# Attention and two feed-forward layers on one core: Q and K of eight tiles as whole rows, memory scores as own products, a new order

## The chip, the cores and the metric

The kernel runs on one core of one Trainium2 chip. The metric is the device time of one execution in microseconds (us). Engines are named as in the profile: PE is TensorE's matmul, PEld its weight load, DVE is VectorE, ACT is ScalarE, POOL is GpSimd, and SP is the engine whose queue issues most of the transfers.

## What is computed

Chunked attention with memory keys on q, k, v of 4 batches x 8 heads x 768 positions x 64, then two feed-forward layers on 3072 tokens x 512, with a hidden width of 2048.

```
for c in range(S // 32):
    k_full = concat(mem_k (8 keys), k[32c - 16 : 32c + 32 + 8])
    v_full = concat(mem_v, v[the same])
    a = softmax(q[chunk c] @ k_full.T / 8)
    out[chunk c] = a @ v_full
x = out as (3072, 512)
x = softplus(x @ w_in) @ w_out
h = x @ w2_in
out = (max(h, 0) + alpha * min(h, 0)) @ w2_out
```

## The kernel before

**Numbers.** All dense products are exact to about float32: each operand is split into a high and a low part in PE's float32r format, and a product is high x high + high x low + low x high. The weights come as 64-bit doubles (`load_raw`, tile `raw`, 512 KB each) and are turned into float32 (tile `word`) by integer operations on DVE: `magnitude` (ab), `clamp` (cl), `convert_a`, `convert_b`, `convert_c` (ca, cb, cv). A high part is then a cast on ACT (wh), and a low part a subtraction on DVE (wl), into `wsplit`.

**Tiles and steps.** Attention is cut into 24 tiles of 128 queries (t = 0 to 23). A tile has scores on PE (`a_scores`, s, into `ps_s` or, from tile 8 on, `ps_a`), a row maximum (m), a shift or bias (c) and an exp (e, on ACT), a sum (n), its reciprocal (r) and the scaling (w), a transpose on PE (t) with its copy (pt, on ACT), the products with V (v*), and a high and a low part of the result (xh on ACT, xl on DVE) into the tile `x`. Four tiles make a block of 512 tokens. The first layer then runs in 96 steps: step i is `h i` (12 products of `x` with a weight block into `ps_hh`, tile `wsplit`), a softplus on ACT (sp, tile `ta`), its high and low part (hi on ACT, lo on DVE, tile `g`), and for the first 64 steps `out i` (12 products into `ps_o`). Steps 0 to 3 use block 0, so `h 0` needs the four tiles 0 to 3; steps 4 to 7 use block 1. Tiles 8 to 23 run between later steps. In the same stretch the weights of layer 2 are converted (ab2, cl2, cv2), split and stored back to memory. From about 495 us on the second layer follows, with seven block products in place of eight (`ps_q`).

**The loads of a tile.** In memory, row p of `qk[t]` holds for one of 128 partitions 1024 floats for Q and 4 x 160 for K: 6656 bytes. Partitions 0 to 63 hold even heads, 64 to 127 odd ones, and of the 1024 floats for Q only every second run of 64 is used, the other is zero. `load_q` (line 424) takes the used runs in two transfers of 64 partitions, `load_k` (line 429) K in a third. K's 160 columns hold the keys of two halves of a tile and the 8 memory keys in between (from column 88). `a_mem` (line 466, km) copies the memory keys on POOL to both ends of K's room, so that each chunk of 32 queries finds its 64 keys in one piece:

```
for e in range(2):
    pe.matmul(ps[at:at + CHUNK, g, u, :], lhsT=q[rows, ...],
              rhs=k_t[t][rows, g, KEYS[j]:KEYS[j] + KW], ...)
```

`load_v` (line 440) brings V of a tile in six transfers of 8, 56 or 64 rows.

**What sets the order.** Each engine's instructions are in a fixed order (`InOrder`). `schedule` (line 1102) gives every piece an engine, a cost, a due time, what it comes after and what rooms it takes; `Plan.run` (line 129) picks the next piece by due times, which are shifted by the offsets in the table `O`. For the opening, up to the sixth step, `OPENING` (line 96) writes the order out, engine by engine. Into PE's planned gaps of the first 90 us `keep_busy` (line 272) puts fillers, products of the zero tile that nobody reads. The planner charges 1.3 us for a change between the exp and the softplus table on ACT, for the pieces that name a table.

Of the kernel before, what the change touches and what calls it, by code (L numbers as in the profile page):

```python
# [11 lines left out]
ALU = mybir.AluOpType  # L12
# [21 lines left out]
MEM0 = SW - NMEM  # L34
KEYS = (0, NMEM + CHUNK, NMEM + 2 * CHUNK, KN - KW)
# [36 lines left out]
class InOrder:  # L72
# [5 lines left out]
    def __getattr__(self, name):  # L78
# [14 lines left out]
O = {'km': -67.99, 's': 76.27, 'm': 79.39, 'c': 26.14, 'e': 113.6, 'n': -26.07, 'r': -9.25, 'w': -103.69, 't': 93.99, 'pt': 7.83, 'v': -16.75, 'xh': 47.66, 'xl': -21.96, 'first': 40.59, 'gap': 81.03, 'second': -74.43, 'gap2': -33.65, 'raw': -107.74, 'ab': 35.37, 'cl': -63.78, 'ca': 12.95, 'cb': 130.93, 'cc': -95.51, 'wh': 81.65, 'wl': 56.47, 'odd': 73.44, 'sp': -41.74, 'hi': 56.35, 'lo': 40.29, 'out': 11.14, 'wait': 0.13, 'sloads': -155.21, 'km0': -117.22, 'km1': 25.05, 's0': 21.36, 's1': 46.75, 'm0': -88.99, 'm1': 60.17, 'c0': 12.89, 'c1': -122.81, 'e0': 101.82, 'e1': -91.77, 'n0': 6.01, 'n1': -115.72, 'r0': 23.2, 'r1': 81.11, 'w0': 40.81, 'w1': -130.46, 't0': 13.18, 't1': -36.53, 'pt0': -117.94, 'pt1': 5.34, 'v0': 51.02, 'v1': -82.24, 'xh0': -60.84, 'xh1': -81.21, 'xl0': 64.94, 'xl1': 45.67, 'by0': -46.78, 'by1': 30.48, 'va': -12.2, 'vb': 88.29, 'vc': 56.73, 'vd': -102.87, 'ra': 33.94, 'rb': 14.7, 'rc': 127.17, 'wld': 105.54, 'dra': -108.27, 'ca0': 58.14, 'ca1': -5.43, 'so': -164.69, 'sq': -8.86, 'sr': -75.99, 'sc': -117.58, 'gn': 46.22, 'l2': -197.81, 'gh': -1.03, 'gl': 116.66, 'ev': -85.64, 'gs': -141.72, 'wo': 68.04, 'yo': 44.51, 'h4': 201.96, 'ac': 53.11}  # L93
# [16 lines left out]
        m 0, corners, c 0, m 1, m 2, n 0, r 0, ab 0, c 1, c 2, m 3, w 0, cl 0, n 1, c 3, r 1, ca 0, cb 0, ab 1, n 2, cl 1, cv 0, r 2, w 1,  # L110
        ca 1, n 3, ab 2, r 3, w 3, cb 1, cl 2, cv 1, ca 2, cb 2, w 2, xl 0, wl 0, m 4, c 4, cv 2, xl 1, n 4, r 4, wl 2, m 5, xl 3, c 5, xl
        2, ab 3, cl 3, wl 1, n 5, ca 3, cb 3, cv 3, r 5, m 6, c 6, lo 0, wl 4, ab 4, cl 4, m 7, ca 4, c 7, cb 4, n 6, cv 4, ab 5, cl 5, ca
        5, cb 5, r 6, cv 5, xl 4, wl 6, n 7, lo 1, ab 6, r 7, cl 6, xl 5, ca 6, wl 3, cb 6, ab 7, cv 6, cl 7, lo 2, ca 7, wl 5, cb 7, xl 6,
# [120 lines left out]
def attention_mlp_mlp_kernel(ctx: ExitStack, tc, qk, v, w1, w2, consts, out):  # L234
# [139 lines left out]
    def low_part(eng, t):  # L374
        eng.tensor_tensor(out=t[1], in0=t[1].bitcast(F32), in1=t[0].bitcast(F32), op=ALU.subtract)
# [30 lines left out]
    raw_q, k_t, v_t, st, s_room = {}, {}, {}, {}, {}  # L406
# [7 lines left out]
    def room_qk(t):  # L414
        if t < 2 * TB:
            room = wpool.tile([P, 4 * DM], F32, tag="w", name="qk0")
            raw_q[t] = room[:, :QN // 2]
            k_t[t] = room[:, QN:QN + NPAIR * KN].rearrange("p (g k) -> p g k", k=KN)
        else:
            room = apool.tile([P, QN // 2 + NPAIR * KN], F32, tag="qk", name="qk", bufs=1)  # L420
            raw_q[t] = room[:, :QN // 2]
            k_t[t] = room[:, QN // 2:].rearrange("p (g k) -> p g k", k=KN)

    def load_q(t, e):
        part = slice(e * D, (e + 1) * D)
        rows = qk[t][part, :QN].rearrange("p (n e k) -> p n e k", e=2, k=D)[:, :, e]
        sp.dma_start(out=raw_q[t][part].rearrange("p (n k) -> p n k", k=D), in_=rows)
# [50 lines left out]
    def a_scores(t):  # L478
        q = raw_q[t].rearrange("p (n k) -> p n k", k=D)
# [27 lines left out]
    def a_max(t):  # L507
# [6 lines left out]
        for rows, w, at, on in ((slice(0, D), 0, slice(NMEM, NMEM + LEFT), i == 0),  # L514
                                (slice(D, P), 1, slice(LEFT + CHUNK, LEFT + CHUNK + RIGHT), i == TPB - 1)):
# [586 lines left out]
    def schedule(when):  # L1102
# [64 lines left out]
        def tile(t, prev, due, step=None):  # L1167
            start, few = t < TB, t >= 2 * TB

            def when_due(k):  # L1170
                return O[k if few else k + "01"[t >= TB]]
# [291 lines left out]
```

## Time and profile before

| what | value |
|---|---|
| time, median of 3 runs | 1075.3 us (1073.28 to 1078.04) |
| the profiled execution | 1077.0 us, its span 1075.2 us |
| PE busy | 1052.6 us, 98% |
| DVE, ACT, POOL busy | 793.8, 559.4, 160.4 us (74%, 52%, 15%) |
| mean granted clock | 0.995 |
| read from and written to memory | 169.42 MB, 60.82 MB |
| chain that ended last | PE 93%, DMA 2%, SP's queue 2%, DVE 1% |

The span is the time from the first to the last instruction. A share is of the span. A line number says nothing here: every engine call runs through the helper in line 80, so rows are told apart by tile names (`ps_hh<-x,wsplit` is an h step). PE's granted clock is a share of 2.4 GHz.

### The profile page before, as it was taken

What the parts mean: (1) busy time and instruction counts of PE and PEld (TensorE: products, weight loads), DVE (VectorE), ACT (ScalarE), POOL (GpSimd) and SP (SyncE); (2) the same over time, 40 slices, a digit from 0 to 9 for tenths busy, and PEclk for the clock granted to TensorE, in tenths of its full rate; (3) what the DMA queues carried; (4) which work ended last, traced back from release to release, by engine and by line L of the source; (5) the groups of instructions that cost most, each with busy time, mean ns of one, the idle gap of its engine ahead of it and who ended that gap; (6) DMA issues with size and microseconds to landing.
All of it is one profiled execution on the core that took longest, in us unless ns stands there. A gap on an engine that the chain in (4) does not pass through costs nothing.

```text
span 1075.2 us, 18801 instructions
## 1 busy us (share of the span) xinstructions
PE 1052.6 (98%) x7229; PEld 860.0 (80%) x7233; DVE 793.8 (74%) x1318; ACT 559.4 (52%) x957; POOL 160.4 (15%) x178
## 2 busy tenths in 40 slices
PE   6899999999999999999999999999999999999998
PEld 3688888887878888878878888888888888888886
DVE  5899995876766788876467766769666879566976
ACT  3564444454543555553355565655465655456543
POOL 0110110431222442235420000000000000000000
PEclk8999999999999999999999999999999999999999
DMA  9876699978657576773999564899875999856804
GB/s 212 221 202 221 169 237 298 232 223 224 202 189 228 181 249 197 255 230 122 357 308 279 217 245 130 309 284 292 203 288 177 342 298 254 265 200 253 362 1 79
DMA packets 171705, 248.25 MB, mean 231 GB/s; under 512 B 79328, under 2 KB 123488, under 8 KB 162400
## 3 DMA queue, kind: packets, MB, share of 16 engines
q1 hardware_dynamic: 166736, 225.95, 65.0%
q0 software_dynamic: 4608, 20.97, 10.0%
q8 instruction: 57, 0.93, 0.4%
q14 instruction: 32, 0.26, 0.1%
q10 hardware_dynamic: 272, 0.13, 0.0%
HBM read 169.42 MB, written 60.82 MB: 214 GB/s over the span
## 4 chain that ended last, share of the span: by engine, by line
PE 93%; DMA 2%; SPq 2%; DVE 1%; issue 1%; ACT 0%; POOL 0%
PE ps_q L80 49%; PE ps_hh L80 24%; PE ps_o L80 16%; PE ps_a L80 3%; SPq L80 2%; DMA qk<-in_qk_dram 1%; DMA raw<-in_w_dram 1%; DMA v<-in_v_dram 1%; PE ps_x L80 0%; DVE g L80 0%; DVE pt L80 0%; PE ps_s L80 0%; ACT g L80 0%; DVE sm L80 0%; PE ps_t L80 0%
## 5 line engine op out<-in xcount | busy, mean ns | idle before, releaser
L80 PE MATMUL ps_q<-g,wout 128*128 128x512 f32 x1344 | 306.9, 390 | 0.8 <-DVE g L80 0.8
L80 PEld LDWEIGHTS ps_q<-g,wout 128*128 128x128 f32 x1344 | 251.9, 188 | 54.6 <-DVE g L80 2.3
L80 PE MATMUL ps_hh<-x,wsplit 128*128 128x512 f32 x1152 | 277.1, 393 | 0.2 <-DVE x L80 0.2
L80 PEld LDWEIGHTS ps_hh<-x,wsplit 128*128 128x128 f32 x1152 | 215.7, 189 | 47.3 <-issue 1.6
L80 PE MATMUL ps_q<-xop,win 128*128 128x512 f32 x1008 | 229.0, 389 | 0.0
L80 PEld LDWEIGHTS ps_q<-xop,win 128*128 128x128 f32 x1008 | 189.3, 188 | 39.2
L80 DVE TENSOR_TENSOR g<-gb,g 128x512 fp32r<-128x512 f32 x224 | 154.6, 702 | 56.2 <-ACT g L80 54.5
L80 ACT CAST g<-gb 128x512 fp32r<-128x512 f32 x224 | 133.0, 621 | 117.3 <-PE ps_q L80 94.9
L80 PE MATMUL ps_o<-g,wsplit 128*128 128x512 f32 x768 | 187.7, 394 | 0.0
L80 PEld LDWEIGHTS ps_o<-g,wsplit 128*128 128x128 f32 x768 | 142.5, 188 | 30.1
L80 ACT ACTIVATE ta<-ps_hh 128x512 f32<-128x512 f32 x88 | 52.6, 598 | 121.9 <-PE ps_hh L80 118.8
L80 DVE SCALAR_TENSOR_TENSOR word<-raw,word 128x512 int32<-128x512 int32 x128 | 94.6, 739 | 2.7
L80 DVE TENSOR_TENSOR g<-ta,g 128x512 fp32r<-128x512 f32 x64 | 49.8, 778 | 41.4 <-ACT g L80 41.3
L80 ACT ACTIVATE tp<-gb 128x512 f32<-128x512 f32 x48 | 30.4, 633 | 90.6 <-DVE gb L80 90.6
L80 DVE SCALAR_TENSOR_TENSOR gb<-gb,tp 128x512 f32<-128x512 f32 x48 | 33.2, 692 | 45.5 <-ACT tp L80 45.5
L80 POOL TENSOR_TENSOR wst<-word,wst 128x512 fp32r<-128x512 f32 (+2 forms) x40 | 44.6, 1119 | 138.6 <-ACT wst L80 129.6
L80 POOL DMA_DIRECT2D gb<-gb x16 | 13.8, 862 | 322.9 <-DVE g L80 302.3
L80 DVE TENSOR_SCALAR word<-word 128x512 int32<-128x512 int32 (+1 forms) x128 | 54.9, 438 | 1.7
L80 ACT CAST g<-ta 128x512 fp32r<-128x512 f32 x64 | 39.7, 621 | 26.5 <-PE ps_o L80 25.8
L80 ACT ACT_TABLE_LOAD x36 | 46.2, 1283 | 3.5 <-PE ps_hh L80 2.2
L80 DVE TENSOR_SCALAR word<-raw 128x512 int32<-128x512 int32 x64 | 39.1, 611 | 8.2 <-DMA raw<-in_w_dram 8.2
L80 POOL TENSOR_TENSOR wst<-wst 128x1024 fp32r<-128x1024 f32 x16 | 41.0, 2565 | 21.1 <-ACT wst L80 16.8
(98 smaller groups left out, 919.9 us busy)
## 6 DMA issues: line engine op xcount, KB each, us to landing
wout<-out_ops SPq DMA_DIRECT2D x42, 1024.0 KB
raw<-in_w_dram SPq DMA_DIRECT2D x64, 512.0 KB
win<-in_ops SPq DMA_DIRECT2D x24, 1024.0 KB
win<-in_ops SPq DMA_DIRECT2D x24, 768.0 KB
gb<-gb POOLq DMA_DIRECT2D x16, 1024.0 KB, 13.2
wout<-outs SPq DMA_DIRECT2D x14, 1024.0 KB
in_ops<-wst SPq DMA_DIRECT2D x24, 512.0 KB
outs<-wst SPq DMA_DIRECT2D x16, 512.0 KB
```

The source lines that it names most:

```text
L80: i = getattr(self.engine, name)(*args, **kw)
```

## The change

Tiles 0 to 7 load Q and K as whole rows, 128 x 6656 bytes in one transfer, zeros included (`load_rows`). K stays as it lies in memory, without room at the ends. For them the scores of the first and the last chunk of a tile become two products each, one with 56 keys and one with the 8 memory keys where they lie (`WINDOWS`); the copies on POOL go. V's rows and the masked columns follow the new order of keys. Tiles 8 to 23 load and multiply as before. Layer 2's magnitude moves from DVE to ACT (`magnitude_by_act`), POOL's low parts run in two halves, some of the planner's costs are others, and `O` and `OPENING` hold new values.

```
+FEW = KW - NMEM
+WINDOWS = (((0, 0, FEW), (FEW, MEM0, NMEM)), ((0, CHUNK, KW),), ((0, 2 * CHUNK, KW),), ((0, MEM0, NMEM), (NMEM, KT - FEW, FEW)))
...
+    def magnitude_by_act(layer, k):
+        m = words[layer, k] = tpool.tile([P, DM], F32, tag="word", name="word", bufs=3)
+        act.activation(out=m, in_=raws[layer, k][:, :, 1].bitcast(F32), func=AF.Abs)
...
     def low_part(eng, t):
-        eng.tensor_tensor(out=t[1], in0=t[1].bitcast(F32), in1=t[0].bitcast(F32), op=ALU.subtract)
+        for n in (slice(0, 2), slice(2, 4)) if eng is pool else (slice(0, 4),):
+            eng.tensor_tensor(out=t[1][:, n, :], in0=t[1][:, n, :].bitcast(F32), in1=t[0][:, n, :].bitcast(F32), op=ALU.subtract)
...
         if t < 2 * TB:
-            room = wpool.tile([P, 4 * DM], F32, tag="w", name="qk0")
-            raw_q[t] = room[:, :QN // 2]
-            k_t[t] = room[:, QN:QN + NPAIR * KN].rearrange("p (g k) -> p g k", k=KN)
+            room = rows_of[t] = wpool.tile([P, 4 * DM], F32, tag="w", name="qk0")
+            raw_q[t] = room[:, :QN].rearrange("p (n e k) -> p n e k", e=2, k=D)
+            k_t[t] = room[:, QN:QK].rearrange("p (g k) -> p g k", k=KT)
...
+    def load_rows(t):
+        sp.dma_start(out=rows_of[t][:, :QK], in_=qk[t])
...
-                        pe.matmul(
-                            ps[at:at + CHUNK, g, u, :], lhsT=q[rows, u * NPAIR + g, c * CHUNK:(c + 1) * CHUNK],
-                            rhs=k_t[t][rows, g, KEYS[j]:KEYS[j] + KW], start=True, stop=True,
-                        )
+                        for to, key, many in WINDOWS[j]:
+                            pe.matmul(
+                                ps[at:at + CHUNK, g, u, to:to + many], lhsT=q[rows, u * NPAIR + g, e, c * CHUNK:(c + 1) * CHUNK],
+                                rhs=k_t[t][rows, g, key:key + many], start=True, stop=True,
+                            )
...
-            add(("ab2", j), "DVE", 0.35, due - 1, lambda j=j: magnitude(1, halves[j]), [("raw2", j)] + ([("ab2", j - 1)] if j else []), ["word"])
+            add(("ab2", j), "ACT", 0.62, due - 1, lambda j=j: magnitude_by_act(1, halves[j]), [("raw2", j)] + ([("ab2", j - 1)] if j else []), ["word"])
...
-        qk 0 2, i raw 0, i v
-        0, i raw 1, i q 4 0, i q 4 1, i raw 2, i v 1, i qk 4 2, i q 5 0, i q 5 1, i v 3, i qk 5 2, i v 2, i raw 3, i q 6 0, i q 6 1, i qk 6
...
+        i qk 0 2, i qk 1 2, i qk 2 2, i raw 0, i qk 3 2, i cst, i raw 1, i v 1, i raw 2, i v 3, i qk 4 2, i v 0, i qk 5 2, i v 2, i raw 3, i
+        qk 6 2, i qk 7 2, i raw 4, i v 4, i raw 5, i v 5, i raw 6, i v 6, i raw 7, i v 7, i raw 8, i raw 9, i raw 10, i raw 11, i q 8 0, i q
```

**SP, the start of its queue.** `qk_103` is tile 0's room before and `qk_102` the change's; the other qk names are tiles 1 to 3, `raw` is a weight block, `cst` the constants, `v_116` the room of a tile's V. Before:

```order
L80 DMA qk_103<-in_qk_dram 64x8x64 x2
L80 DMA qk_103<-in_qk_dram 128x4x160
L80 DMA qk_101<-in_qk_dram 64x8x64
L80 DMA qk_100<-in_qk_dram 64x8x64
L80 DMA qk_101<-in_qk_dram 64x8x64
L80 DMA qk_100<-in_qk_dram 64x8x64
L80 DMA qk_101<-in_qk_dram 128x4x160
L80 DMA cst<-in_consts_dram 128x144
L80 DMA qk_102<-in_qk_dram 64x8x64 x2
L80 DMA qk_100<-in_qk_dram 128x4x160
L80 DMA qk_102<-in_qk_dram 128x4x160
L80 DMA raw<-in_w_dram 128x512
```

Now:

```order
L82 DMA qk_102<-in_qk_dram 128x1664
L82 DMA qk_103<-in_qk_dram 128x1664
L82 DMA qk_100<-in_qk_dram 128x1664
L82 DMA raw<-in_w_dram 128x512
L82 DMA qk_101<-in_qk_dram 128x1664
L82 DMA cst<-in_consts_dram 128x144
L82 DMA raw<-in_w_dram 128x512
L82 DMA v_116<-in_v_dram 56x512
```

Twelve transfers for four tiles became four, the first weight block stands ahead of tile 3's rows, and the second ahead of all of V. Further down, V comes in the order of tiles 1, 3, 0, 2, with the rows of tiles 4 and 5 in between.

**PE, the scores of tile 0.** Before, they are one run of products behind the fillers:

```order
L80 MATMUL ps_s<-zero 128x512
L80 MATMUL ps_s<-qk_103 32x64 x32
L80 LDWEIGHTS zero
L80 MATMUL ps_s<-zero 128x512
```

Now the end of tile 0's and the start of tile 1's:

```order
L82 MATMUL ps_s<-qk_102 32x64 x4
L82 MATMUL ps_s<-qk_102 32x8
L82 MATMUL ps_s<-qk_102 32x56
L82 MATMUL ps_s<-qk_102 32x8
L82 MATMUL ps_s<-qk_102 32x56
L82 LDWEIGHTS zero
L82 MATMUL ps_s<-zero 128x512
L82 MATMUL ps_s<-qk_103 32x56
```

32 products in the program became 48 a tile, and five fillers between tiles 0 and 1 became one.

**ACT, between two h steps of the middle.** `ta<-ps_hh` is a step's softplus, `g<-ta` its high part, `pt<-pt` a tile's exp. Before, around the first V products of tile 8:

```order
L80 ACTIVATE ta<-ps_hh 128x512
L80 CAST g<-ta 128x512
L80 CAST wst<-word 128x256
L80 ACT_TABLE_LOAD
L80 ACTIVATE pt<-pt 128x512
L80 ACT_TABLE_LOAD
L80 ACTIVATE ta<-ps_hh 128x512
```

Now, at the same place:

```order
L82 ACT_TABLE_LOAD
L82 ACTIVATE word<-raw 128x512
L82 ACT_TABLE_LOAD
L82 ACTIVATE ta<-ps_hh 128x512
L82 CAST g<-ta 128x512
L82 CAST wst<-word 128x256
L82 CAST x<-ps_a 128x4x128
L82 ACTIVATE ta<-ps_hh 128x512
L82 CAST g<-ta 128x512
L82 ACT_TABLE_LOAD
L82 ACTIVATE word<-raw 128x512
```

The magnitude (`word<-raw`) came to ACT, and the compiler put a table load ahead of it and one behind. ACT's whole list has 84 table loads, 36 before.

## Rows read from the trace of the kernel before

**Rows 1.** The page, busy us (share of the span) and instructions of each engine.
```profile
PE 1052.6 (98%) x7229; PEld 860.0 (80%) x7233; DVE 793.8 (74%) x1318; ACT 559.4 (52%) x957; POOL 160.4 (15%) x178
```
**Rows 2.** Waits of PE: us in total, times, longest.
```profile
PE ps_s L80 <- POOL qk L80: 5.3, 5, 2.0
PE ps_a L80 <- issue: 3.4, 2, 2.2
PE ps_s L80 <- issue: 3.1, 3, 2.6
```
**Rows 3.** Timeline of PE, 0 to 62: start, us, operation, [idle before].
```profile
6.46 1.12 PE L80 MATMUL ps_s<-qk 64*32 64x64 f32 x64 [2.04 <-POOL qk L80]
...
17.32 1.34 PE L80 MATMUL ps_s<-qk 64*32 64x64 f32 x52 [2.63 <-issue]
...
31.41 1.20 PE L80 MATMUL ps_x<-pt,v 128*64 128x64 f32 x32
...
38.98 2.79 PE L80 MATMUL ps_hh<-x,wsplit 128*128 128x512 f32 x11 [0.22 <-DVE x L80]
43.81 0.41 PE L80 MATMUL ps_s<-qk 64*32 64x64 f32 x12 [2.04 <-POOL qk L80]
...
45.52 4.40 PE L80 MATMUL ps_hh<-x,wsplit 128*128 128x512 f32 x12
...
55.34 3.02 PE L80 MATMUL ps_hh<-x,wsplit 128*128 128x512 f32 x12
```
**Rows 4.** Windows: stretch, length; PE, PEld, DVE, ACT, POOL busy; PEclk, DMA share, GB/s.
```profile
0.00:14.72 14.72, 10.14 (x219) 5.29 (x222) 4.00 (x13) 3.23 (x10) 1.87 (x14) 0.88 0.91 211
...
20.00:30.00 10.00, 8.02 (x93) 4.99 (x92) 9.79 (x26) 6.04 (x20) 1.12 (x2) 0.94 0.88 197
...
40.00:50.00 10.00, 7.76 (x95) 5.66 (x97) 7.56 (x16) 5.73 (x8) 2.16 (x5) 0.83 0.97 237
```
**Rows 5.** Windows chosen by what the DMA queue moved.
```profile
3.00:9.00 6.00, 3.62 (x71) 1.85 (x71) 1.29 (x4) 0.00 (x0) 0.35 (x2) 0.88 1.03 207
...
15.00:24.00 9.00, 6.35 (x72) 3.66 (x72) 6.84 (x20) 5.74 (x25) 0.00 (x0) 0.81 1.08 225
...
48.00:60.00 12.00, 12.00 (x169) 9.66 (x168) 9.86 (x21) 6.21 (x11) 1.23 (x1) 0.98 0.86 235
90.00:102.00 12.00, 12.00 (x55) 9.94 (x54) 11.93 (x25) 5.31 (x9) 0.00 (x0) 1.00 0.53 170
```
**Rows 6.** Timeline of SP, 0 to 40.
```profile
0.74 5.42 SPq L80 DMA_DIRECT2D qk<-in_qk_dram  x8
...
13.97 0.37 SPq L80 DMA_DIRECT2D raw<-in_w_dram  x1
```
**Rows 7.** Timeline of DVE, 0 to 40.
```profile
18.75 0.69 DVE L80 TENSOR_REDUCE nm<-ps_s 128x8 f32<-128x512 f32 x1 [2.02 <-PE ps_s L80]
19.36 0.68 DVE L80 TENSOR_TENSOR v<-v,r 128x512 f32<-128x512 f32 x1
...
38.24 0.69 DVE L80 TENSOR_TENSOR x<-ps_x,x 128x512 fp32r<-128x512 f32 x1
```
**Rows 8.** The page, DMA queues: packets, MB, share of 16 engines.
```profile
q8 instruction: 57, 0.93, 0.4%
```
**Rows 9.** Groups of ACT instructions: busy us, mean ns, idle before.
```profile
L80 ACT ACT_TABLE_LOAD x36 | 46.2, 1283 | 3.5 <-PE ps_hh L80 2.2 <-PEq L1453 0.7
L80 ACT CAST g<-ta 128x512 fp32r<-128x512 f32 x64 | 39.7, 621 | 26.5 <-PE ps_o L80 25.8
...
L80 ACT CAST wst<-wst 128x1024 fp32r<-128x1024 f32 x24 | 25.0, 1048 | 10.0 <-DVE wst L80 8.1 <-POOL wst L80 1.4 <-DMA qk<-in_qk_dram 0.5
```
**Rows 10.** Timeline of ACT, 455 to 500.
```profile
473.81 1.28 ACT L80 ACT_TABLE_LOAD   x1
...
477.20 0.60 ACT L80 ACTIVATE ta<-ps_hh 128x512 f32<-128x512 f32 x1
```
**Rows 11.** Timeline of PE, 455 to 500.
```profile
470.08 11.18 PE L80 MATMUL ps_hh<-x,wsplit 128*128 128x512 f32 x48
```

More of the change, by code (lines that the diff above doesn't have):

```diff
@@ L108 @@
+        4
     """,
     "DVE": """
[L110 to L113, printed above, removed]
@@ L125 @@
+        8 1, i raw 12, i raw 13, i qk 8 2, i v 8, i raw 14
     """,
@@ L426, in load_q @@
         rows = qk[t][part, :QN].rearrange("p (n e k) -> p n e k", e=2, k=D)[:, :, e]
-        sp.dma_start(out=raw_q[t][part].rearrange("p (n k) -> p n k", k=D), in_=rows)
+        sp.dma_start(out=raw_q[t][part], in_=rows)
     def load_k(t):
@@ L478, in a_scores @@
     def a_scores(t):
[L479 removed]
+        q = raw_q[t]
         if t < 2 * TB:
@@ L513, in a_max @@
                  apool.tile([P, SLOTS, 1], F32, tag="sm", name="sm", bufs=2))
-        for rows, w, at, on in ((slice(0, D), 0, slice(NMEM, NMEM + LEFT), i == 0),
-                                (slice(D, P), 1, slice(LEFT + CHUNK, LEFT + CHUNK + RIGHT), i == TPB - 1)):
+        near, far = (NMEM, LEFT + CHUNK) if few else (0, NMEM + LEFT + CHUNK)
+        for rows, w, at, on in ((slice(0, D), 0, slice(near, near + LEFT), i == 0),
+                                (slice(D, P), 1, slice(far, far + RIGHT), i == TPB - 1)):
             if on:
@@ L1182, in tile @@
             add(("qr", t), "", 0.0, soon, room, free_qk, qrooms)
-            for e in range(2):
+            for e in range(2 if few else 0):
                 dma(("q", t, e), 0.66, 0.67, soon, lambda e=e: load_q(t, e), [("i", "q", t, 0) if e else ("qr", t)])
-            dma(("qk", t, 2), 0.65, 1.4, soon, lambda: load_k(t), [("i", "q", t, 1)])
+            if few:
+                dma(("qk", t, 2), 0.65, 1.4, soon, lambda: load_k(t), [("i", "q", t, 1)])
+            else:
+                dma(("qk", t, 2), 0.38, 2.4, soon, lambda: load_rows(t), [("qr", t)])
             add(("vr", t), "", 0.0, soon + 2, lambda: room_v(t), [("i", "qk", t, 2)] + ([("i", "v", prev)] if few else []), vrooms)
             dma(("v", t), 2.9, 2.0, (O["va"], O["vb"], O["vc"], O["vd"])[t] if start else due - 24, lambda: load_v(t), [("vr", t)])
-            add(("km", t), "POOL", 0.36, due - when_due("km"), lambda: a_mem(t), [("qk", t, 2)])
-            after_s = [("km", t)] + [("q", t, e) for e in range(2)] + [("qk", t, 2)] + ([("s", prev)] if prev >= 0 else [])
+            if few:
+                add(("km", t), "POOL", 0.36, due - when_due("km"), lambda: a_mem(t), [("qk", t, 2)])
+            after_s = ([("km", t)] + [("q", t, e) for e in range(2)] if few else []) + [("qk", t, 2)] + ([("s", prev)] if prev >= 0 else [])
             after_s += ([("v*", t - 2)] if t >= 2 * TB + 2 else []) + ([("t", TB - 1)] if t == TB else []) + ([("pt", prev)] if t > 2 * TB else []) + ([("h", step)] if step else [])
@@ L1198, in tile @@
             else:
-                add(("s", t), "PE", 0.9 if few else 1.09, due - when_due("s"), lambda: a_scores(t), after_s, [] if start else ["pair", "s"] if few else ["pa"], qrooms)
+                add(("s", t), "PE", 0.9 if few else 1.3, due - when_due("s"), lambda: a_scores(t), after_s, [] if start else ["pair", "s"] if few else ["pa"], qrooms)
             add(("m", t), "DVE", 0.75 if t % TPB in (0, TPB - 1) else 0.62, due - when_due("m"), lambda: a_max(t), [("s", t)] + ([] if few else [("vr", t)]) + ([("xh", prev)] if joint else []))
@@ L1265, in schedule @@
                 raw, eng, name = U < EARLY, *((pool, "POOL") if U >= BYPOOL else (dve, "DVE"))
-                add(("sums2", q, z), name, 3.2 if name == "POOL" else 1.65, due + 3, lambda q=q, z=z, eng=eng, raw=raw: weight_sums(q, z, eng, raw),
+                add(("sums2", q, z), name, 3.2 if name == "POOL" else 2.0, due + 3, lambda q=q, z=z, eng=eng, raw=raw: weight_sums(q, z, eng, raw),
                     [("cv2", j)] + ([("sh2", (U - 1) // 2, (U - 1) % 2, 4)] if U else []), ["raw"] * 1 if raw else ["w"])
@@ L1281, in schedule @@
             rooms = ["w"] if q else ["raw"] * 2
-            add(("rc", q), "DVE", 1.4, due - O["sq"], lambda q=q: whole_again(q), [("wl", 4 * q + 1), ("wl", 4 * q + 3), ("raw", 2 * NF - 1)] + ([("sl1", q - 1)] if q else []), rooms)
+            add(("rc", q), "DVE", 1.2, due - O["sq"], lambda q=q: whole_again(q), [("wl", 4 * q + 1), ("wl", 4 * q + 3), ("raw", 2 * NF - 1)] + ([("sl1", q - 1)] if q else []), rooms)
             add(("sums1", q), "DVE", 1.65, due - O["sr"], lambda q=q: sums_of_first(q), [("rc", q)])
```

36 lines of the change are left out of this document (18 added, 18 removed).

## The prediction

> **What bounds the kernel now.** I read the busy shares first, then the windows by stage, then TensorE's waits, and only then the opening's rows. TensorE (PE) is busy for 1052.6 of 1075.2 us [rows 1], so all that can be won is its 22.6 us of idle time, its fillers and its slow stretches. The waits name 5.3 us for the copies of memory keys on POOL, and 3.1 and 3.4 us under "issue", where the engine waited for nothing that the profile shows [rows 2]. They are all in or near attention products. The chain of waits says the same: 93% of the span is PE, and nothing behind the opening leads away from it for long. So the end is set by when the first dense step (h 0) can run, plus what PE loses after it.
>
> In the opening's timeline h 0 runs its last eleven products from 38.98 on, s 6 then waits 2.04 us for its Q and K rows, and h 1, behind that hole, takes 4.40 us where a later step takes 3.02 [rows 3]. The granted clock in 40 to 50 is 0.83 of 2.4 GHz, where 1.00 is the rule [rows 4]: part of that stretch ran at the 1.2 GHz level, and PE had been idle before. VectorE (DVE) is busy for 9.79 of the 10 us from 20 to 30 [rows 4], so it is nearly a second bound there. The third is the DMA queue: shares near 1 in 3 to 9 and 15 to 24 [rows 5].
>
> **The change, part by part.** Q and K of a tile: three transfers (two of 131 KB in pieces of 256 B, one of 328 KB in pieces of 640 B; 0.59 MB) become one of 0.852 MB in pieces of 6656 B, since the zeros between come along. Issues: eight of the old ones take 5.42 us, 0.68 each; one over 128 whole rows takes 0.37, as a raw load does [rows 6]. For the eight tiles that is 24 x 0.68 - 8 x 0.37 = 13 us less on the SP queue, but it pays only where the queue, not the bytes, is late. Bytes: in 3 to 9, almost only small pieces, 207 GB/s at share 1.03 are 201 GB/s for a full share; in 90 to 102, raw loads of 4 KB pieces alone, 170 at 0.53 are 321; in 48 to 60, raw and V by turns, 235 at 0.86 are 273 [rows 5]. The rows of the change are nearest to raw loads, so I take 321: 2.65 us a tile against 0.59 / 0.201 = 2.93 before. The slow end is 208 (225 at 1.08, the mixed stretch 15 to 24), 4.1 us; the raw stretch is itself the fast one. So each tile gains little by itself. A raw load is 1.63 us, and V's 0.524 MB is then 2 x 0.524 / 0.273 - 1.63 = 2.2.
>
> When is h 0 ready? It needs tile 2's values, whose V is the last load. In the change's queue six Q/K rows, three raw loads, four V and the constants go up to it: 15.9 + 4.9 + 8.8 + 0.2 = 29.8 us. Start and completion: s 0 began at 6.46, behind a copy of 0.35 on POOL, so 0.59 MB had landed 5.4 us after the first issue at 0.74; less 2.9 for the bytes that is 2.5. V of tile 2 lands at 0.74 + 2.5 + 29.8 = 33.0; values 1.2, high part 0.6, low part 0.7 and three hand-overs bring h 0 to 35.7, against 38.98.
>
> DVE is the other condition. From max 3 (18.75) to the last low part (38.24 + 0.69) it now takes 20.2 us. The change's list has, behind max 3, 22 passes at 0.61 from start to start [rows 7], 6 word passes at 0.37, 4 reciprocal pairs at 0.33 and one bias: 17.1 us. Max 3 needs tile 3's rows, fifth in the queue: 0.74 + 2.5 + 4 x 2.65 + 1.63 = 15.5, then s 3 and the max, 2.2: 17.7. DVE is then done at 34.8.
>
> The memory keys lose the copies (5.3 us of waits as printed), and the scores of a tile go from 64 to 96 products in hardware. Before, 64 take 1.12 us [rows 3]; the ends are no cost (the added ones have 8 columns) and half again, 0.56. I take 1.5 us a tile, since they come as pairs with weight loads of the same size. In the opening this hides in waits for rows; for s 6 and s 7, behind h 0, it costs 0.8 us.
>
> These products are instructions too, and here the row speaks against the change. At 14.7 PE stopped in the middle of s 2 for 2.63 us with its operands there, after 219 + 222 instructions [rows 3, 4]. 57 instruction transfers of 0.93 MB served 7229 + 7233 instructions, some 254 each [rows 1, 8]: as I read it, PE had used up its block. The change reaches the same count early in s 2 and the next block's end in s 3, only some 5 us later, while the queue is full. Ends: no stall, or two of 2.63 in a row. I take one before max 3. DVE's chain is then done at 34.8 + 2.6 = 37.4, later than the loads' 35.7, and sets h 0: 1.6 us sooner than now (38.98). The Trainium skill (Runtime: NRT & Kernel Launch, Instruction fetch mechanics) says that crossing into a new block of instructions is mostly hidden; the trace here disagrees, with 2.63 us. By that rule h 0 would be ready at 35.7.
>
> Behind h 0: the 2.04 us wait of s 6 goes, since its rows follow V of tile 2 by 1.63 + 2.65 us and h 0 covers 2.8 and its own start 1 us more; s 6 and s 7 cost 0.8; the slow step stays, only it is now h 0, since PE has few fillers and long waits between 20 and 37. That is 2.0 - 0.8 = 1.2.
>
> Layer 2's magnitudes go from DVE to ScalarE (ACT) as Abs, 32 passes. An activation on such a tile takes 0.60 (the row of 477.20 below). PE's waits hardly name DVE there, so its relief brings nothing. But the compiled list has 84 table loads where there were 36, mostly a load on either side of an Abs. At 1.28 us [rows 9] 48 more are 61.6 us on ACT, which stood at 52% [rows 1]. Is it hidden? At 473.81 a load, an exp and a load made an activation start at 477.20, 1.3 us behind its step, and PE ran through its 48 products without a gap [rows 10, 11]. An Abs between two loads is as long (3.2 us). From the end of h(i) to out(i) there are two blocks of 2.72, less activation 0.60, high part 0.62 [rows 9], low part 0.70 and 0.2 for hand-overs: 3.3 us of slack. So a bare pair fits; a gap with an exp, an Abs and a cast of 1.05 [rows 9] (4.9 us) overruns by some 0.7 where dense steps follow each other, and few are like that. I take 1.0 us, between 0 and 11 (below). The Trainium skill (ScalarE: Activation LUTs, Table sets: the hidden batching unit) lists abs as filler in every table set; by that none of the 48 would be needed and this 1.0 would be 0, but the compiled list has them.
>
> The two halves of a POOL subtraction add 16 instructions to an engine that is busy for 15% [rows 1]. The other due times leave the number of attention runs among dense steps at 48, and the 3.4 us of "issue" in attention pairs [rows 2] move rather than go: nothing.
>
> **Sum.** 1.6 + 1.2 - 1.0 = 1.8 us off the profiled execution (1077.0, which is 1.7 above the median of 1075.3 and 1.8 above its own span). Against the median: **1073.5 us**. The forecast's own range, 1070 to 1077, is the stall at 0 to 5.2 and the loads at 0 to 3. About 0.5%, or 5.4 us, is what a measurement of this kernel can tell from no change: 1069.9 and 1080.7.
>
> **Rivals.**
> 1. The opening gains in full: no instruction stall, and PE at 2.4 GHz into h 0. Then 3.3 (h 0 at 35.7) + 1.2 + 1.4 (4.40 against 3.02) and no loss to loads is 5.9: 1069.4; up to 3 more if the attention pairs' 3.4 us of "issue" fall where no block ends. For it: the gaps between tiles, 2.65 us each by the rows' bytes, give time to fetch. Against: the denser code.
> 2. The rows are no faster, so the transfer doesn't do what it is for. At 240 GB/s over all, 8.85 MB take 36.9 us, V of tile 2 lands at 40.1 and h 0 is at 42.8, 3.9 later; with the other terms 3.9 - 1.2 + 1.0 = 3.7 slower: 1079.0. For it: 15 to 24 shows 208, with raw and V in it.
> 3. Slower: table loads reach PE. The gaps that hold an Abs pair and also a 1.05 us cast or two drains number about 13 in the compiled list; if each pays its overrun, 0.85 on average, that is 11 us, where I took 1: 1083.4. It decides as soon as ACT's list between two steps is longer than PE's 5.44 plus the 3.3 of slack carried over. For it: the planner's costs hold no load for Abs. Against: [rows 10, 11].
>
> **How the numbers follow.** Forecast 0.47, rival 1 0.27, rival 2 0.13, rival 3 0.13. The range of 8 in 10 takes in the forecast, rivals 1 and 2 with their bounds: 1066.5 to 1080. Faster by over 0.5%: rival 1 and a little of the forecast's low end, 0.29; slower: rival 3, 0.13; within: 0.58.
>
> **What will show it.** The new trace should have h 0's last products from 37 on (35.5 for rival 1, over 41 for rival 2), an "issue" wait in s 2 or s 3, no wait in s 6 and no copies on POOL; 84 table loads, with PE's idle from 150 to 550 not above 5 us. If ACT is named as releaser of ps_o or ps_hh there, rival 3 is right. The forecast is wrong if h 0 comes after 39 or if PE's idle time moves behind 60 us.

## The result, and the profile after

The changed kernel takes 1082.72 us, median of six runs (1081.59 to 1086.6); the kernel before took 1077.51 beside it (six runs, 1073.28 to 1079.27). The ratio, taken over all runs and not of the medians, is 1.0059, 95% interval 1.0034 to 1.0083: about 6.3 us slower (5.2 by the medians), where 1.8 us faster was forecast and the range ended at 1080. The profiled execution took 1086.6 us, span 1084.8; it is the slowest of the six.

The page of the changed kernel: busy time by engine, the instruction queue, and the table loads (busy, mean ns, idle before).

```profile
PE 1057.3 (97%) x7472; PEld 864.6 (80%) x7476; DVE 774.6 (71%) x1286; ACT 640.7 (59%) x1037; POOL 161.1 (15%) x178
...
q8 instruction: 59, 0.97, 0.4%
...
L82 ACT ACT_TABLE_LOAD x84 | 107.8, 1283 | 2.2 <-PEq L1468 0.7
```

PE has 4.7 us more of busy time than before and 243 more products [rows 1]; ACT has 84 table loads for 36 [rows 9]. The waits of PE say where idle time went (us in total, times, longest):

```profile
PE ps_x L82 <- issue: 4.6, 2, 2.6
PE ps_s L82 <- issue: 3.1, 4, 2.0
PE ps_hh L82 <- ACT gb L82: 2.7, 1, 2.7
...
PE ps_hh L82 <- ACT ta L82: 2.5, 3, 1.1
```

The 5.3 us for POOL's copies [rows 2] are gone. New are 4.6 us under "issue" in products with V (`ps_x`), and 5.2 us for ACT in h steps (`ps_hh`). The first lie in the opening; timeline of PE (start, us, operation, count, idle before):

```profile
5.52 2.27 PE L82 MATMUL ps_s<-qk 64*32 64x56 f32 x96 [2.63 <-DMA qk<-in_qk_dram]
...
10.57 0.51 PE L82 MATMUL ps_s<-qk 64*32 64x56 f32 x25 [0.25 <-issue]
13.11 1.68 PE L82 MATMUL ps_s<-qk 64*32 64x56 f32 x71 [2.03 <-issue]
...
31.84 0.68 PE L82 MATMUL ps_x<-pt,v 128*64 128x64 f32 x15
35.09 1.13 PE L82 MATMUL ps_x<-pt,v 128*64 128x64 f32 x17 [2.57 <-issue]
36.15 2.27 PE L82 MATMUL ps_s<-qk 64*32 64x56 f32 x96
38.35 1.11 PE L82 MATMUL ps_x<-pt,v 128*64 128x64 f32 x14
41.45 1.36 PE L82 MATMUL ps_x<-pt,v 128*64 128x64 f32 x18 [1.99 <-issue]
...
43.72 4.83 PE L82 MATMUL ps_hh<-x,wsplit 128*128 128x512 f32 x12
48.48 1.37 PE L82 MATMUL ps_s<-qk 64*32 64x56 f32 x96
```

The rows arrive in time and s 6 (48.48) does not wait. But PE stops three times in the middle of a run of products, for nothing that the profile shows: at 11.1, 32.5 and 39.5. h 0 begins at 43.72, where before its last eleven products ran from 38.98 [rows 3]. That is over 41, the sign that the prediction gave for rows that are no faster (rival 2); but here the rows were in time and the stops stand in front of h 0. The windows of the same kernel (length; PE, PEld, DVE, ACT, POOL busy; granted clock, DMA share, GB/s) give the clock:

```profile
3.00:9.00 6.00, 3.01 (x130) 2.90 (x134) 0.31 (x2) 0.00 (x0) 0.00 (x0) 1.00 1.00 411
...
30.00:40.00 10.00, 6.44 (x172) 5.48 (x168) 5.67 (x13) 4.03 (x10) 1.04 (x1) 0.69 1.00 315
40.00:50.00 10.00, 8.55 (x132) 6.96 (x133) 5.45 (x12) 5.89 (x11) 1.04 (x1) 0.63 0.85 225
150.00:440.00 290.00, 288.40 (x2895) 235.73 (x2894) 203.18 (x334) 201.46 (x266) 85.41 (x96) 1.00 0.76 226
440.00:540.00 100.00, 94.72 (x709) 76.39 (x708) 51.40 (x85) 66.83 (x88) 38.24 (x42) 0.98 0.62 206
520.00:530.00 10.00, 7.55 (x27) 6.15 (x28) 3.21 (x5) 4.27 (x7) 1.84 (x2) 0.83 0.95 339
```

The clock from 30 to 50 is 0.69 and 0.63 of 2.4 GHz: after the stop at 32.5 it is at 0.50, the 1.2 GHz level, from 34 to 47, and h 0 takes 4.83 us. DVE, at 9.79 from 20 to 30, is at 5.67 in the next ten: it waits for PE now (4.20 us before 38.55). The other loss lies in 440 to 540: PE is busy for 94.72 us of 100, and from 150 to 440 it loses next to nothing. PE's rows there:

```profile
440.94 2.88 PE L82 MATMUL ps_o<-g,wsplit 128*128 128x512 f32 x12
443.66 2.89 PE L82 MATMUL ps_hh<-x,wsplit 128*128 128x512 f32 x12
...
460.66 5.74 PE L82 MATMUL ps_hh<-x,wsplit 128*128 128x512 f32 x24 [0.66 <-ACT ta L82]
...
480.92 5.75 PE L82 MATMUL ps_hh<-x,wsplit 128*128 128x512 f32 x24 [0.83 <-ACT ta L82]
...
500.38 19.34 PE L82 MATMUL ps_hh<-x,wsplit 128*128 128x512 f32 x84 [1.05 <-ACT ta L82]
522.45 15.21 PE L82 MATMUL ps_hh<-x,wsplit 128*128 128x512 f32 x60 [2.73 <-ACT gb L82]
```

The first row is the last out step: behind it, h steps follow each other with only pieces of attention between them, one every 2.72 us. Four waits make 5.27 us. Behind the longest the clock falls (0.83 over ten us in the window above, 0.50 from 522.4 to 525.2): the 60 products there take 15.05 us up to 537.50, where five steps of 2.72 are 13.6, another 1.4. What ACT did before 522.45:

```profile
517.46 1.06 ACT L82 CAST wst<-wst 128x1024 fp32r<-128x1024 f32 x1 [2.49 <-POOL wst L82]
518.54 1.28 ACT L82 ACT_TABLE_LOAD   x1
519.83 0.66 ACT L82 ACTIVATE word<-raw 128x512 f32<-128x512 f32 x1
520.51 1.28 ACT L82 ACT_TABLE_LOAD   x1
521.80 0.60 ACT L82 ACTIVATE gb<-ps_hh 128x512 f32<-128x512 f32 x1
```

A cast waits 2.49 us for POOL, then come the cast and an Abs between two loads, 4.3 us, and only then the activation that frees the room of an h step. The wait for POOL alone is not enough: with the Abs away and POOL's halves kept (e6, e13) PE has no such wait.

### The profile page after: what moved, and what is told of

Read it like the earlier page. It is cut to its first block, busy times and chain, and to the rows that moved or that the text cites. A ratio compares the mean times of both kernels' runs of the same rounds, so it can differ in the third digit from the quotient of the medians.

```text
span 1084.8 us, 19323 instructions
## 1 busy us (share of the span) xinstructions
PE 1057.3 (97%) x7472; PEld 864.6 (80%) x7476; DVE 774.6 (71%) x1286; ACT 640.7 (59%) x1037; POOL 161.1 (15%) x178
## 4 chain that ended last, share of the span: by engine, by line
PE 90%; DVE 3%; ACT 3%; issue 2%; DMA 1%; POOL 1%; SPq 0%; ACTq 0%; DVEq 0%; POOLq 0%
PE ps_q L82 48%; PE ps_hh L82 21%; PE ps_o L82 16%; PE ps_a L82 3%; ACT L82 1%; DVE word L82 1%; PE ps_s L82 1%; PE ps_x L82 1%; POOL wst L82 1%; DMA win<-in_ops 1%; SPq L82 0%; DMA qk<-in_qk_dram 0%; DVE g L82 0%; ACT ta L82 0%; ACT word L82 0%
## 5 line engine op out<-in xcount | busy, mean ns | idle before, releaser
L82 PE MATMUL ps_hh<-x,wsplit 128*128 128x512 f32 x1152 | 280.6, 396 | 5.3 <-ACT gb L82 2.7
L82 DVE TENSOR_TENSOR g<-gb,g 128x512 fp32r<-128x512 f32 x224 | 156.9, 712 | 52.8 <-ACT g L82 50.9
L82 DVE SCALAR_TENSOR_TENSOR word<-raw,word 128x512 int32<-128x512 int32 x128 | 92.1, 719 | 2.5
L82 DVE TENSOR_SCALAR word<-word 128x512 f32<-128x512 f32 (+1 forms) x128 | 59.5, 474 | 47.8 <-ACT word L82 46.9
L82 POOL TENSOR_TENSOR wst<-wst 128x512 fp32r<-128x512 f32 x32 | 46.2, 1508 | 28.8 <-ACT wst L82 21.0
L82 ACT COPY tc<-ps_q 128x512 f32<-128x512 f32 x48 | 26.6, 596 | 17.9 <-PE ps_q L82 17.9
```

The lines of the kernel that those rows point to most:

```text
L82: i = getattr(self.engine, name)(*args, **kw)
```

## The experiments

The theory after this reading has two parts. **(A)** Instructions: PE stops where a block of them is used up, and the 16 more products a tile (32 in hardware) bring it there sooner, while the DMA queue is full. **(B)** Table loads reach PE, but only in the stretch of h steps without out steps. Rivals: the whole rows or DVE set h 0; the loads are hidden; the new order itself is worse. Below, "tail" is the span less the start of h 4, which cuts the opening off: kernel before 1075.2 - 71.07 = 1004.1, changed 1084.8 - 74.28 = 1010.5. All ratios are against the kernel before, run on the same chip beside it.

| run | ratio (95%) | h 4 at | tail |
|---|---|---|---|
| changed kernel | 1.0059 (1.0034 to 1.0083) | 74.28 | 1010.5 |
| e1_no_loads | 0.9987 (0.9976 to 0.9999) | 70.14 | 1001.3 |
| e2_ends | 0.9998 (0.9986 to 1.001) | 65.15 | 1009.5 |
| e3_extra | 1.0053 (1.003 to 1.0075) | 73.10 | 1005.0 |
| e4_abs_act | 1.0482 (1.0459 to 1.0505) | 71.47 | 1057.4 |
| e6_dve_abs | 0.9991 (0.998 to 1.0001) | 70.07 | 1002.8 |
| e7_dve_abs_ends | 0.9923 (0.991 to 0.9935) | 63.91 | 1001.7 |
| e8_compact | 0.9911 (0.9898 to 0.9924) | 63.40 | 1001.6 |
| e9_rows_old_order | 0.9958 (0.9946 to 0.9971) | 67.16 | 1003.6 |
| e10_pad | 0.9991 (0.9975 to 1.0007) | 70.49 | 1001.7 |
| e11_v_rows | 0.9906 (0.9889 to 0.9922) | 63.16 | 1001.9 |
| e12_abs_old_order | 1.0081 (1.0057 to 1.0105) | 68.01 | 1013.3 |
| e13_late_dve | 1.0001 (0.9983 to 1.0019) | 71.68 | 1001.8 |

### The changed kernel without table loads (e1)

```
-        act.activation(out=m, in_=raws[layer, k][:, :, 1].bitcast(F32), func=AF.Abs)
+        act.copy(out=m, in_=raws[layer, k][:, :, 1].bitcast(F32))
```

> The changed kernel with layer 2's 32 magnitudes on ScalarE as plain copies, in the same places of the same order; the copy needs no table, so the 48 extra table loads are gone. It leaves out the absolute value. Theory (two costs: PE's instruction stalls in the opening, and table loads that reach PE in the middle): PE's four waits on ACT at 460 to 525 (5.3 us) and the slow stretch behind the longest go, h 4 still starts at 74, so the time is 4 to 8 us below the changed kernel's. Rival (loads are hidden, everything is lost in the opening): within 1.5 us of the changed kernel.

Measured: 0.9987, 7.2 thousandths (7.8 us) below the changed kernel, and the tail falls by 9.2 us to 1001.3. In the profile three of the four waits on ACT are gone and 0.7 us of them is left. The loads cost PE time; "hidden" falls. (That they do so only in one stretch is for e13.) h 4 came at 70.1, where 74 was expected: this execution has only one late stop, in the V products of tile 2 (3.28 us), so the profiled run of the changed kernel had the worse opening of the two.

### The changed kernel with 32 products a tile (e2)

```
+QK = QN + NPAIR * KN
...
-                        for to, key, many in WINDOWS[j]:
-                            pe.matmul(
-                                ps[at:at + CHUNK, g, u, to:to + many], lhsT=...,
-                                rhs=k_t[t][rows, g, key:key + many], ...)
+                        pe.matmul(
+                            ps[at:at + CHUNK, g, u, :], lhsT=...,
+                            rhs=k_t[t][rows, g, KEYS[j]:KEYS[j] + KW], ...)
```

(In memory each K row then has the memory keys at both ends too; V's rows and the masked columns are those of before.)

> The changed kernel with the memory keys laid in memory at both ends of each K row (6912 bytes a row in place of 6656), so that a tile's scores are 32 products in the program again and no copies are needed; table loads stay. Theory (denser products meet the end of an instruction block twice while the queue is full): the first stall moves back behind the first V products or away, the one in the V products of tiles 3 or 2 goes, h 0 runs its last products 2 to 5 us earlier than 43.7, and the time is 2 to 5 us below the changed kernel's. Rival (whole rows are too slow for the queue and DVE sets h 0, products do not matter): h 0 stays within 1 us and the time within 1 us, or above it by the 4 per cent more bytes.

Measured: 0.9998, 6.1 thousandths below the changed kernel, more than expected. h 0's last eleven products run from 37.19, where in the changed kernel all twelve started at 43.72, though each row is 4% longer. So neither the rows nor DVE had set h 0. The tail stays long, at 1009.5: the two costs lie in different stretches.

### The kernel before with 16 more products a tile (e3)

```
+                        if j in (0, 3):
+                            pe.matmul(
+                                ps[at:at + CHUNK, g, u, :NMEM], lhsT=...,
+                                rhs=k_t[t][rows, g, KEYS[j]:KEYS[j] + NMEM], ...)
```

> The kernel before with the memory keys' scores of tiles 0 to 7 computed a second time, as 16 products of 8 columns more a tile at the first and last chunk, and nothing else changed. Theory (the instructions, not the columns, cost): one more issue wait of 2 to 3 us stands in PE's opening, h 0 comes 2 to 4 us after 39.0, and the time is 2 to 5 us above the kernel before. Rival (48 products a tile cost only their columns, some 0.4 us a tile, hidden in waits for rows): within 1 us of the kernel before, h 0 within 0.5 us.

Measured: 1.0053, some 5.7 us above the kernel before, just over the upper end of what A gave. Timeline of PE:

```profile
16.07 0.80 PE L80 MATMUL ps_s<-qk 64*32 64x64 f32 x44 [0.15 <-DMA v<-in_v_dram]
18.89 1.50 PE L80 MATMUL ps_s<-qk 64*32 64x64 f32 x52 [2.02 <-issue]
...
33.30 0.39 PE L80 MATMUL ps_x<-pt,v 128*64 128x64 f32 x5
35.31 1.03 PE L80 MATMUL ps_x<-pt,v 128*64 128x64 f32 x27 [1.63 <-issue]
...
36.86 1.37 PE L80 MATMUL ps_s<-qk 64*32 64x64 f32 x95
40.55 0.17 PE L80 MATMUL ps_s<-qk 64*32 64x8 f32 x1 [2.32 <-issue]
```

There are two stops more than before, 1.63 and 2.32, and h 0's eleven products run from 43.75 in place of 38.98. A tile's scores take 1.40 for 1.12 us, 0.28 more; for the six tiles up to h 0 that is 1.7 of the 4.8, part of it hidden in waits for rows. So most of the price is the stops, in the old order and with the old transfers too.

### Does the place move with the count? (e10)

```
             pe.matmul(ps, lhsT=zero, rhs=zero[:, :1].to_broadcast([P, N2]), start=True, stop=True)
+        for _ in range(60 if name == ("s", 0) else 0):
+            pe.matmul(ps[:, :NMEM], lhsT=zero, rhs=zero[:, :NMEM], start=True, stop=True)
```

> The changed kernel with magnitudes on DVE (36 table loads), and 60 products of 8 columns that nobody reads put into PE's idle 2.6 us before the scores of tile 0. Theory (a stall falls where a fixed count of PE's instructions is used up, 220 products and then every 127, so the place in the program moves by 60): the first issue stall moves from 25 products into s 2 to 60 products into s 1 and lasts until 12 to 14 us; the one in the V products of tile 2 goes, and others stand, if anywhere, 90 products into s 4 or 53 into s 5. Rival (the stalls belong to their places, to tile 2's rows or V): both stay where they are, 25 into s 2 and 14 into the V products of tile 2.

Measured: 0.9991, the same as e6 below, which is this kernel without the 60. Timeline of PE:

```profile
8.16 1.73 PE L82 MATMUL ps_s<-qk 64*32 64x56 f32 x62 [0.47 <-issue]
11.30 1.02 PE L82 MATMUL ps_s<-qk 64*32 64x64 f32 x34 [1.42 <-issue]
12.80 2.05 PE L82 MATMUL ps_s<-qk 64*32 64x56 f32 x93 [0.47 <-issue]
17.50 0.29 PE L82 MATMUL ps_s<-qk 64*32 64x8 f32 x3 [2.65 <-issue]
...
36.19 0.84 PE L82 MATMUL ps_s<-qk 64*32 64x56 f32 x51
38.42 0.79 PE L82 MATMUL ps_s<-qk 64*32 64x8 f32 x45 [1.39 <-issue]
```

The stops came where A had put them: 62 products into s 1 (60 expected) and 51 into s 5 (53), with the one in tile 2's V products gone, and one more after 93 of s 2. Only the first one's end was missed: 11.30, before the 12 to 14 expected. Counted from the start, PE stopped after 222, 349 and 726 products here; after 221, 598 and 725 in the changed kernel (4 + 96 + 96 + 25 from the rows above and those between); after 347, 596 and 722 in e3; after 219 in the kernel before. That is one grid, 220 and every 126 or so from there, and 126 products with as many weight loads are 252 instructions: the 254 of an instruction transfer that [rows 1, 8] gave. So the place is a matter of the count. The trace of the changed kernel also holds the transfers themselves. In the windows 10:11, 19:20, 32:33 and 38:39 (each 1 us; a share of 6.4% of 16 engines is 1.0 us on one) the DMA queues have:

```profile
q8 instruction: 1, 0.02, 6.4%
q8 instruction: 1, 0.02, 6.8%
q8 instruction: 1, 0.02, 7.5%
q8 instruction: 1, 0.02, 5.5%
```

Three of them start at 10.6, 32.4 and 39.0, less than 0.5 us before PE stops, and PE goes on 1.4 to 1.6 us after each has ended. The one at 19.5 comes some 9 us ahead of 474 products (28.6), and there PE does not stop. In e13 the transfer for 725 starts at 36.3, 1.1 us after PE has stopped, and the stop is the longest, 3.69 us. So a transfer takes about 1 us, and what differs is when it starts. A crossing does not always stop PE: 474 never did in these four, but e2, e8, e9 and e11, with 32 products a tile, have 0.3 to 1.6 us at 469 to 472. What makes a transfer start late, the full queue or the pace of the instructions, was not tried apart.

### Magnitudes back on DVE, in the changed kernel's order (e6), and both undone (e7)

```
-            add(("ab2", j), "ACT", 0.62, due - 1, lambda j=j: magnitude_by_act(1, halves[j]), ...
+            add(("ab2", j), "ACT", 0.62, due - 1, lambda j=j: magnitude(1, halves[j]), ...
```

e7 has this and the edit of e2.

> The changed kernel with layer 2's magnitudes issued on DVE, as integer shifts like before, at the very places of the order where the Abs stood; 36 table loads. Theory (the loads cost some 7 us, the DVE passes are free because DVE has room there): ratio to the kernel before 0.998 to 1.001, like the run with plain copies, and no waits on ACT at 460 to 525. Rival (DVE needed the relief: 32 passes of 0.35 us before the clamps make PE wait for converted words or low parts): ratio over 1.002, with PE waits on DVE between 150 and 560.

> The changed kernel with both taken back: memory keys at both ends of each K row (32 products a tile) and the magnitudes on DVE. Theory (two costs in different stretches add): 1.0059 - 0.0061 - 0.0072 = 0.9926 of the kernel before, some 1068.5 us; h 4 starts at 65 to 67 and the stretch behind it is as long as in the run with plain copies (1001 us). Rival (the two overlap, or time won in the opening is lost again to a late weight): 0.996 or more.

Measured: 0.9991 and 0.9923 (1068.50 us). No wait on ACT from 60 us on, and none on DVE but the 1.0 or 1.1 us in the second layer that the kernel before has as well (0.8): the passes are free on DVE. With e6 as base the products' price is 0.9991 - 0.9923 = 6.8 thousandths, 7.3 us; the loads' price is 1.0059 - 0.9991, the same 7.3; by the intervals each may be off by 2 to 3 us. For both together 0.9926 was expected. In e7's timeline of PE h 0 is at 35.95, at full clock, and s 6 and h 1 follow without a hole:

```profile
35.95 2.79 PE L82 MATMUL ps_hh<-x,wsplit 128*128 128x512 f32 x11 [0.22 <-DVE x L82]
38.67 1.10 PE L82 MATMUL ps_s<-qk 64*32 64x64 f32 x64
39.70 3.06 PE L82 MATMUL ps_hh<-x,wsplit 128*128 128x512 f32 x12
```

### Only the last ten magnitudes on DVE (e13)

```
+            ... lambda j=j: (magnitude if j >= 22 else magnitude_by_act)(1, halves[j]), ...
```

> The changed kernel with only the last ten of the 32 magnitudes (those from 430 us on, where h steps follow each other without an out step between) issued on DVE; the first 22 stay on ScalarE as Abs, with their table loads (66 left). Theory (loads are hidden as long as an out step stands between two h steps, and reach PE only behind step 64): as good as with all 32 on DVE, ratio 0.998 to 1.001, no waits on ACT behind 430. Rival (each load costs a little everywhere): about two thirds of the loss stays, ratio 1.003 to 1.005.

Measured: 1.0001, 0.9983 to 1.0019: within what the theory gave, and the rival's 1.003 is outside the interval. The windows of this run show it by stretch:

```profile
150.00:440.00 290.00, 288.83 (x2898) 236.21 (x2897) 206.08 (x338) 199.99 (x265) 85.71 (x97) 1.00 0.77 226
440.00:540.00 100.00, 99.63 (x739) 81.34 (x738) 58.69 (x93) 42.06 (x65) 46.69 (x47) 1.00 0.66 221
```

With 66 loads left and 22 Abs, PE loses 1.2 us from 150 to 440 (1.6 in the changed kernel, all of it under "issue") and only 0.4 us, not 5.3, from 440 to 540. The tail is 1001.8, as short as with no extra load at all (1001.3 and 1002.8 in e1 and e6). Of the 48 added loads 30 were free within the noise; the other 18, with the last ten Abs, made the cost.

### Abs on ScalarE in the kernel before (e4, e12)

```
-            add(("ab2", j), "DVE", 0.35, due - 1, lambda j=j: magnitude(1, halves[j]), ...
+            add(("ab2", j), "ACT", 0.62, due - 1, lambda j=j: magnitude_by_act(1, halves[j]), ...
```

e12 changes the call alone and leaves the plan "DVE", 0.35.

> The kernel before with layer 2's magnitude as an Abs on ScalarE in place of DVE, with the cost that the changed kernel's planner gives it. Theory (table loads between softplus steps reach PE): table loads rise from 36 to about 84, PE has waits on ACT of 3 to 8 us in all between 150 and 560, and the time is 3 to 8 us above the kernel before. Rival (hidden by ScalarE's free share): within 1.5 us of the kernel before.

> The kernel before, its plan unchanged, with layer 2's magnitudes issued on ScalarE as Abs at the places where DVE had them; DVE is freed of them, table loads come with them. It separates the loads from the reshuffled order of the earlier try. Theory (loads between softplus steps reach PE whatever the order): ratio 1.003 to 1.010, PE waits on ACT or on what ACT feeds between 150 and 560 of 3 to 9 us. Rival (the loads hurt only in the changed kernel's own order): within 0.0015 of 1.

Measured: 1.0482 and 1.0081. e4 missed by far and answers another question: with another cost the planner made another order of everything behind the opening. Its PE waits:

```profile
PE ps_a L80 <- DVE pt L80: 16.9, 3, 8.3
PE ps_q L80 <- ACT g L80: 9.1, 2, 6.4
```

Before the longest of each, ACT itself had been idle, for DVE (6.0 us) and for POOL (3.5 us): no load stands there. With the plan kept, e12 shows the Abs with their loads: 80 loads, 8.7 us by the ratio, tail 1013.3 against 1004.1, and the same kind of wait in the same stretch, 4.5 us in all (the rest of the tail's 9.2 is not taken apart here):

```profile
516.02 16.62 PE L80 MATMUL ps_hh<-x,wsplit 128*128 128x512 f32 x72 [3.00 <-ACT gb L80]
```

### The transfer alone (e9), and fewer bytes (e8, e11)

e9 is the kernel before with load_q empty for tiles 0 to 7, a_mem too, and

```
+            sp.dma_start(out=rows_of[t][:, :QK], in_=qk[t])
```

e8 is e7 with rows of 512 floats for Q in place of 1024; e11 is e8 with V laid out as needed:

```
-                sp.dma_start(out=v_t[t][to:to + n, part], in_=v[t][at:at + n, part])
+            sp.dma_start(out=v_t[t], in_=v8[t])
```

> The kernel before, in its own order and with its own due times, with Q, K and the memory keys at both ends of tiles 0 to 7 as whole rows of 6912 bytes in one transfer, and without the copies on POOL; products and everything else stay. Theory (the transfer alone is good, the new order adds to it): POOL waits of 5.3 us go, h 0 comes 1 to 3 us before 39.0, s 6 does not wait, the time is 2 to 5 us under the kernel before; the order and due times of the changed kernel then bring the rest. Rival (the transfer brings nothing in the old order, where raw and V come late anyway): within 1 us.

> The same with the zeros left out of Q in memory: rows of 4864 bytes in place of 6912, order the same. Theory (behind the stalls the opening is bound by the queue's bytes: 0.26 MB less a tile at 318 GB/s are 0.8 us, six tiles up to V of tile 2): h 0 0.5 to 3 us earlier than with the zeros and 0.5 to 3 us less in all. Rival (DVE's chain behind max 3 and the instruction blocks set h 0): within 1 us of the run with the zeros.

> The best version so far (compact rows, memory keys at both ends, magnitudes on DVE) with V of tiles 0 to 7 laid in memory as the tile needs it and loaded as 128 rows of 4096 bytes in one transfer in place of six, order unchanged. Theory (between 14 and 18 us V is late behind SP's six issues a tile): t 0 starts 1 to 2.5 us before 17.9 and the time falls by 0.5 to 2 us. Rival (bytes or DVE bound the opening): within 0.7 us of 0.9911 of the kernel before.

Measured: e9 0.9958, 4.5 us below the kernel before, as the theory had it: h 0's eleven products from 37.03 and s 6 without a wait. What else is new in e7 (order, due times, POOL's halves) then brings 0.9958 - 0.9923, 3.8 us, 3.3 of it before h 4. So the order is not to blame. But 1.95 us of those 3.3 is one stop in e9's s 7, at 720 products, where e7 has none: that part may be where the block's end falls, and not the order as such. e8 0.9911: h 0 is 1.4 us earlier (34.58) and the time 1.3 us less, as the theory had it, but within reach of the interval of e7 (0.991 to 0.9935): the zeros cost little. e11 0.9906: t 0 at 17.91, where it was 17.88 in e8, and nothing gained; V was not late because of SP's six issues. e8 and e11 (1066.45 and 1066.84 us) beat the kernel before by 10 us and the changed one by 16.

## Why the prediction was wrong, point by point

**What it read right.** The rows' transfer: s 0 at 5.52 (5.9 by the sum), no wait in s 6, no copies, and by themselves 4.5 us (e9). The two conditions for h 0, 35.7 by loads and 34.8 by DVE, lie near what e7 (35.95) and e8 (34.58) show without the late stops. The 35.7 is partly luck: rows came at 411 GB/s where the sum had 321, some 3 us less for six tiles, and yet the last wait for V of tile 2 ended at 33.87 in e7, where the sum had it landed at 33.0; what took the difference no run shows. Rival 1, the opening in full without a cost for loads, gave 1069.4; e7, which has neither the loads nor the added products, measured 1068.5. The 0.8 us for the longer scores of s 6 and s 7 was near (1.37 against 1.10 each, so 0.5).

**The step that failed first: "So a bare pair fits", few gaps overrun, and "I take 1.0 us".** The loads cost 7.3. The slack of 3.3 us was worked out from h(i) to out(i), with a block between. That holds up to step 63, and there the loads are free (e13). The rows of [rows 10, 11] do lie in the stretch behind, but show one pair of loads around an exp, without an Abs or a cast, and even that made its activation 1.3 us late. From 443.7 on there is no out step: ACT has to serve an h step every 2.72 us, and a 1.05 us cast beside one Abs pair already fills 4.3. The last ten magnitudes, nine of them in that stretch, did the harm, 5.3 us as waits and 1.4 as slow clock. The price of one overrun was right where an exp stands beside the Abs (0.66 and 0.83 us, 0.7 in the prediction); too small were the count and the longest, 2.73 us, where the cast also waited for POOL. Rival 3 had the mechanism, and its sign came (ACT named as releaser of `ps_hh`); but it has 13 gaps over the whole layer, 11 us, where four waits made the cost. That its 1083.4 lies at the measured 1082.72 is luck, since it also counted a gain in the opening that did not come. The rule of the Trainium skill named there (ScalarE: Activation LUTs, Table sets: the hidden batching unit), by which an abs needs no load, fell with the compiled list, and e1 now gives the price of the difference.

**The second: "I take one before max 3", a stop of 2.63 us.** It came (2.03 us). But the count that the prediction had itself (254 instructions a block) was not carried on to the V products, 598 and 725 products in, behind which h 0 hangs. There are one or two late stops, 2.0 to 3.7 us, and, where the sum had a slow step only for want of fillers, a slow clock behind them. In the profiled run that is 4.6 us of stops, and h 0 takes 4.83 us. The products' price is 7.3 us, where the sum had 2.5: 1.7 for the stop (37.4 in place of 35.7) and 0.8 for s 6 and s 7. The opening then gave nothing: h 4 at 70.1 to 71.7 in e1, e6, e10 and e13, whose PE program up to there is the changed kernel's (e10 with 60 more), against 71.07 in the kernel before (68.0 to 71.5 in three executions of that opening).

**The third, on the other side: "The other due times leave ... nothing".** What is new beside rows and products brought 3.8 us (e9 to e7), some 2 of it perhaps by where a block's end falls; with the rows' 4.5 that is 8.3, where the sum had 5.3 before its stop and longer scores (3.3 for h 0 at 35.7 and 2.0 for s 6).

Added up from the runs: rows -4.5, order and due times -3.8, own products +7.3, table loads +7.3, together +6.3 us. That this is what was measured proves nothing: the four are steps on one way from the kernel before over e9, e7 and e6 to the changed one, and have to add up. But pairs off that way agree: 7.8 (e1) and 8.7 us (e12) for the loads, 6.6 (e2) and 5.7 (e3) for the products. The change holds two good parts and two bad ones, and the forecast had each of the bad ones at a fraction of its price: 5.3 - 2.5 - 1.0 = 1.8 us faster, where the runs have 8.3 - 7.3 - 7.3.

## What to carry to other kernels

Slack belongs to a stretch: before calling added work on a side engine hidden, work out its room in each stretch in which the step's rhythm differs, above all where a cover (here the out step) ends. Where many small products run while loads fill the queue, count instructions as well as columns, mark every block's end in the list, and see who hangs on the products behind it. When a change is a bundle, take its parts back one by one in the same order; a planner that is given another cost makes another kernel, which measures something else.

## What the runs showed of the hardware that was not expected

PE's instructions come in blocks of some 254 (59 transfers, 0.97 MB in all, 16 KB each), and a block's end can stop PE for up to 3.7 us in the opening, in the middle of a group of products, when the transfer of about 1 us starts only as PE gets there. The Trainium skill (Runtime: NRT & Kernel Launch, Instruction fetch mechanics) says that the crossing is mostly hidden; in the changed kernel the trace agrees at 474 products, where the transfer came 9 us ahead, and disagrees at 221, 598 and 725.

Rows of 6656 bytes came at 411 GB/s at a full share from 3 to 9, where small pieces gave 201 and raw loads 321, scaled to a full share [rows 5].

The same opening is not equally long in every execution: h 4 at 71.07, 71.47 and 68.01 in the kernel before, e4 and e12, which share it up to there, while the tails of the runs with 36 table loads lie within 1001.3 and 1005.0. So the spread between runs of one kernel may come in great part from the first 70 us; each kernel has one profile here, so this is not shown.
